# Moving work in the front of a gated attention mix: row-maximum units, weight splits, head casts and inversions at other places

## The chip, the cores and the metric

The kernel runs on one core of one Trainium2 chip. Time is device time in microseconds (us) from the first to the last instruction of one execution. The core has TensorE (PE, with its weight loads shown as PEld), VectorE (DVE), ScalarE (ACT), GpSimd (POOL) and SyncE (SP). Each engine works through its own instructions in their order and waits at semaphores. SP issues nearly all DMA transfers; the profile calls its issuing queue SPq.

## The reference, cut to what matters

There are 2048 tokens of width 448, and 16 heads of width 28. Two attention layers share the input, and a gate per token mixes them:

```python
x = A_x                                              # 1 x 2048 x 448
g = sigmoid((x * gate_w).sum(-1))                    # one gate a token
# branch A: linear attention, features by a softmax over each head's 28 columns
pq, pk = q @ w_phi, k @ w_phi                        # per head
phi = concat(softmax(p), softmax(-p))                # 56 features a head
o_a = (phi_q @ (phi_k.T @ v)) / (phi_q @ sum(phi_k) + 1e-6)
# branch B: full softmax attention over all 2048 keys
o_b = softmax(q @ k.T * 28**-0.5) @ v
out = g * (o_a @ wo_A) + (1 - g) * (o_b @ wo_B)
```

## The kernel before, in words

Operands of the projections are split into a high part (rounded to fp32r) and a low part (the rest), and each product is made of three passes: high by high, high by low, low by high. The high part is a cast, the low part a subtraction.

The program has a front, some 334 us long, and a main loop of 256 steps (lines 1123 to 1162) that does the scores, the exponentials and the values of branch B. This change lies in the front.

**The front, in order.** First come 20 projections of queries and keys for branch B (`proj_qk`, n = 4 to 19 at lines 664 to 699). Then one loop (lines 727 to 825) runs i from 0 to 42. For i below 16 it handles the keys and values of branch A for token tile t = i (128 tokens). With q = i - 16 and y = q - 1 it handles the queries of branch A, stage after stage, one tile behind the other:

- query projection `pq` of tile q (q from 0 to 15), copied out of PSUM by ACT;
- `features1` (line 438): the extremes of each head by DVE (lines 443, 444), the two differences by POOL (447) and by POOL or DVE (449); an exponential by ACT (452), one iteration later; `features2` (455): the sums and their inverse by DVE (459, 460) and the product by POOL (461);
- `turn` (515): PE transposes the features of tile y - 2, ACT copies them out (528);
- for each pair of tiles k (256 tokens, 8 pairs): `numer` (531) multiplies with the state, and `normalize1` (395) copies the result `oU` out by ACT and has SP pick the denominators out of it by DMA into `den`; `normalize2` (405) adds 1e-6 and inverts on DVE (408, 409), then SP stores the inverses to DRAM (`rd`, line 413) and loads them back, broadcast to all partitions, into `rs` (line 414); `normalize3` (418) multiplies `oU` by `rs` on DVE (420); `normalize4` (423) casts the heads on ACT (428) and subtracts on POOL (429);
- `out_a` (557): the output projection of branch A for tile y - 10, twelve passes; ACT scales it by the gate (565) and SP stores it;
- `value_b` (712): the value projections of branch B, tiles 0 to 7 inside the loop from q = 18, tiles 8 to 15 behind it (lines 915 to 925).

Pair k is summed up at y = 2k + 4, inverted at y = 2k + 5, multiplied at y = 2k + 8, cast at y = 2k + 9 and projected at y = 2k + 10 and 2k + 11.

**Maxima units.** Branch B needs a bound on the scores of each query for its exponentials. 44 units (`mx_unit`, line 259) find part of these in the front: each is four matmuls on 28 rows (line 285) into the PSUM tiles `pmb` and `pmd`, a Relu by ACT (288) and two add-and-maximum operations by DVE (290), each with a read of its accumulator. A unit's `pmb` is written where the unit before had its own, so PE waits for DVE there. Units stand between other work: at n = 16 to 19, two for each pair of key tiles (one at the start, one by `tick` at half the passes), at q = 0, 1 and from q = 8, and a second one an iteration from q = 19 (line 817) until 44 are done.

**Weight splits.** `split_weight` (line 141) casts the high part on ACT and puts the low part, a subtraction, on a list that `take_lows` empties at the next chance, on DVE unless another engine is named.

**PSUM.** Tiles of 512 columns come from the tag `s` with three buffers, plus one tile `pv` that holds the state of branch A until q = 2 (the turn from keys to queries). There the kernel before closes its PSUM pool and opens another with four `s` buffers (lines 749 to 751).

**What sets the order.** The instructions of PE, DVE, ACT and POOL run in the order in which the program writes them. SP's order is set by the framework's planner. The main loop takes its score tiles from a list of seven PSUM banks (`free`, line 935).

Of the kernel before, what the change touches and what calls it, by code (L numbers as in the profile page):

```python
# [19 lines left out]
D = 448  # L20
# [20 lines left out]
def gated_mix_kernel(ctx, tc, xT, wqkB, wvB, wvA, wkAT, wqAT, phi, woA, woB,  # L41
# [17 lines left out]

    psn = [3, 2]  # L60

    def ps_s(nm):
        return ps.tile([P, 512], F32, tag="s", name=nm, bufs=psn[0])

    def ps_pv(nm):
        return ps.tile([P, 512], F32, tag="pv", name=nm, bufs=1)
# [74 lines left out]
    def split_weight(w, raw, bs, cs, low=nc.vector, high=nc.scalar.copy):  # L141

        high(w[:, 0, bs, cs], raw)
        lows.append(lambda: low.tensor_sub(w[:, 1, bs, cs], raw, f32(w[:, 0, bs, cs])))
# [464 lines left out]
    def part_loads(key, src, n, nm):  # L609
        loads(key, lambda: load_part(src, n, nm, 0), lambda: load_part(src, n, nm, 2))  # L610

    def split_part(w, key, n, i, low=nc.vector):
        split_weight(w, raws[key][i], slice(2 * i, 2 * i + 2), slice(0, n), low)

    def splits(n):

# [47 lines left out]
    for n in range(4, NP):  # L664
        take_acts()
        if n in (4, 5):
            x_loads(n - 2)
        if n == 8:
            nc.sync.dma_start(phi_s, phi)
            load_fold(wkAT, "k")  # L670
        if n == 10:
            part_loads("wB1", wqkB[:, :, 512:896], 384, "wB1")
        splits(n + 1)
        if n == 14:
            part_loads("wvA", wvA, 450, "wvA")
            nc.sync.dma_start(sel_s, sel)
            nc.sync.dma_start(mask_s, mask)
            for v in vap:
                nc.gpsimd.memset(v[:, :, 28:32], 0.0)
                nc.gpsimd.memset(v[:, :, 28:29], 1.0)  # L680
            feats = [bd.tile([P, H, 64], F32, name=f"feat{i}") for i in range(4)]
            for f in feats:
                nc.gpsimd.memset(f[:, :, 56:], 0.0)
        if 16 <= n < 20:
            mx_unit()
        proj_qk(n, ev)
        if n in (16, 18):
            split_part(wvA_s, "wvA", 450, (n - 16) // 2)
            take_lows()
        if 12 <= n < 16:  # L690
            fold(wkA_s, "k", n - 12)
        if n == 10:
            pair_query(0, 0)
            pair_load(0, 0)
        if n == 15:
            pair_load(0, 1)
            pair_query(0, 1)
        if n in (14, 19):
            take_subs()
# [27 lines left out]
    for i in range(2 * NT + 11):  # L727
        t, q = i, i - NT
        y = q - 1
        tb = y // 2  # L730
        take_acts()
        if t < NT and t % 2 == 0:
            mx_unit()
            passes = (55 if t < NT - 4 else 44) + (4 if t >= 4 else 0)
            pace["n"], pace["at"] = 4 if t >= 4 else 0, [passes // 2]
        if q in (0, 1):
            take_exps()

        if t % 2 == 0 and 0 <= t - 4 < NT:
            kv_add(t - 4)  # L740
            kv_add(t - 3)
        if q == 2:
            bk_s.close()
            ta_s = ExitStack()
            ta = ta_s.enter_context(tc.tile_pool(name="ta", bufs=1, reuse_waits="tile"))
            stg = ta_s.enter_context(tc.tile_pool(name="stg", bufs=2, reuse_waits="tile"))
            KV = ta.tile([P, 512], F32, name="KV")
            kvT = kv_copy()
            ps_s_.close()
            ps = ps_s_.enter_context(tc.tile_pool(name="psq", bufs=1, space=PSUM, reuse_waits="tile"))  # L750
            psn[0] = 4
            woA_s = weights(3, "woA_s")
            wvB_s = weights(2, "wvB_s")
            take_exps()
        if t < NT:
            pk = ps_s(f"pk{t}")
            tok_major(pk, t, wkA_s, D, tick)
            fk[t] = features1(pk, f"k{t}", nc.gpsimd)
            take_exps(1)
        if 0 <= q < NT:  # L760
            pq = ps_s(f"pq{q}")
            tok_major(pq, q, wqA_s, D)
        if q == 0:
            fk[NT - 1] = features2(fk[NT - 1], f"k{NT - 1}")
        if q in (1, 2):
            fq[q - 1] = features2(fq[q - 1], f"q{q - 1}")
        if 0 <= q < NT:
            fq[q] = features1(pq, f"q{q}", nc.vector if 0 < q < 9 else nc.gpsimd)
        if 0 <= t - 1 < NT - 1:
            fk[t - 1] = features2(fk[t - 1], f"k{t - 1}")  # L770
        if q in (0, 1) or q >= 8:
            mx_unit()
        if y >= 9 and y % 2 and tb - 4 < 8:
            oTs[tb - 4] = normalize4(ta, num.pop(tb - 4), f"a{tb - 4}", 2)
        if y >= 4 and y % 2 == 0 and tb - 2 < 8:
            numer(tb - 2)
        if q > 0:
            take_exps(int(q < NT))
        if q == 3:
            kv_out(kvT)  # L780
        if 2 <= q - 1 < NT:
            fq[q - 1] = features2(fq[q - 1], f"q{q - 1}")
        take_subs()
        if t == 1:
            pair_load(0, 3)
        if y >= 8 and y % 2 == 0 and tb - 4 < 8:
            num[tb - 4] = normalize3(*num[tb - 4], 2)
        if t < NT:
            value_a(t)
            if t % 2 and t < NT - 4:  # L790
                proj_qk(NP + t // 2, ev)
        if q in (0, 1):
            proj_qk(NP + 6 + q, ev)
        take_lows()
        if 2 <= i < 6:
            fold(wqA_s, "q", i - 2)
        if q == 1:
            ev_s.close()
        if q == 2:
            raws["woA"] = [load_woA(b) for b in (0, 2)]  # L800
        if q == 11:
            part_loads("wvB", wvB, D, "wvB")
        if q in (4, 6):
            split_part(woA_s, "woA", D, (q - 4) // 2)
        if q in (14, 17):
            split_part(wvB_s, "wvB", D, (q - 14) // 3)
        if q == 1:
            gates()
        if y < 9 or y % 2:
            if y >= 2 and y - 2 < NT:  # L810
                turn(y - 2)
        if 0 <= y - 10 < NT:
            out_a(y - 10)
            out_a2(y - 10)
        if y >= 9 and y % 2 == 0 and y - 2 < NT:
            turn(y - 2)
        if NT + 3 <= q < NT + 10:
            mx_unit()
        if q == NT + 2:
            bd_s.close()  # L820
            vb = [value_tile(0)]
        if 0 <= q - NT - 2 < 8:
            value_b(q - NT - 2)
        if y >= 5 and y % 2 and tb - 2 < 8:
            num[tb - 2] = normalize2(ta, *num[tb - 2], f"a{tb - 2}", 2, True)
    ta_s.close()
    wp_s.close()
    vb.append(value_tile(1))
# [80 lines left out]
    ps_s_.close()  # L909
    ps = ps_s_.enter_context(tc.tile_pool(name="psv", bufs=1, space=PSUM, reuse_waits="tile"))  # L910
    psn[:] = 2, 3
    rlp = fr_s.enter_context(tc.tile_pool(name="rlp", bufs=1, reuse_waits="tile"))
    mx_unit()
    rest = NF - mxs["u"]
# [17 lines left out]

    free, used, held = list(range(7)), [], []
    spare = []

    def bank(i, nm):
# [292 lines left out]
```

## Time and profile before

| | |
|---|---|
| three runs | 1019.61, 1020.08 (median), 1020.7 us |
| profiled execution | 1018.93 us, span of its trace 1017.1 us |
| PE busy | 1006.6 us (99%) |
| ACT busy | 817.2 us (80%) |
| DVE busy | 682.1 us (67%) |
| POOL busy | 236.4 us (23%) |
| mean granted TensorE clock | 0.998 |

A row of a timeline has the start in us from the span's begin, the duration in us, the engine, the source line, the operation, and the tile written and those read; xN means that N instructions stand together. A bracket gives the time that the engine was idle just before and what ended that time. A row of the windows has busy us of PE, PEld, DVE, ACT and POOL with their instruction counts, then the granted clock of PE, the busy share of the DMA engines and GB/s. A row of one tile has the smallest, the median and the largest duration in ns, and the first and the last start. A row of waits has the total us, the times, and the longest.

### The profile page before, as it was taken

Reading aid. Unit: us, or ns where it says so; the run is one execution under the profiler, and the core shown is the slowest. Engines: PE = TensorE matmul, PEld = TensorE weight load, DVE = VectorE, ACT = ScalarE, POOL = GpSimd, SP = SyncE. Lnnn points to the kernel's source line nnn. Section 1 sums busy time; section 2 is a strip of 40 time slices with the busy share of each in tenths; the row PEclk is TensorE's granted clock in tenths of the full one; section 3 lists DMA queues with packets and bytes.
Section 4 is the critical chain, followed back from the end, with each engine's and each line's share of the span. In section 5 each row is a group of like instructions: output and inputs, shape, how many; then the busy total and the mean of one; then the engine's idle time right before and its main releaser. Section 6 shows DMA issues by size and latency. Waiting matters only on the chain.

```text
span 1017.1 us, 18036 instructions
## 1 busy us (share of the span) xinstructions
PE 1006.6 (99%) x6472; PEld 563.0 (55%) x6472; DVE 682.1 (67%) x1340; ACT 817.2 (80%) x1534; POOL 236.4 (23%) x213
## 2 busy tenths in 40 slices
PE   9999999999999999999999999999999999999998
PEld 8878888878779433333333333333333333355656
DVE  5566657997753578888887888787887878710102
ACT  5445445677753899999999999999999999978682
POOL 1235456588435102110011110101201011011010
PEclk9999999999999999999999999999999999999999
DMA  8973110132345703232522223532323345516131
GB/s 298 312 236 92 58 52 1 44 90 82 91 131 122 160 14 90 58 80 69 124 68 70 55 58 78 126 68 53 87 55 75 76 100 138 144 48 163 56 111 55
DMA packets 64250, 98.89 MB, mean 97 GB/s; under 512 B 18176, under 2 KB 24944, under 8 KB 64160
## 3 DMA queue, kind: packets, MB, share of 16 engines
q1 hardware_dynamic: 64160, 97.74, 36.0%
q8 instruction: 51, 0.84, 0.3%
q14 instruction: 39, 0.32, 0.1%
HBM read 69.54 MB, written 27.78 MB: 96 GB/s over the span
## 4 chain that ended last, share of the span: by engine, by line
PE 92%; DVE 4%; DMA 1%; ACT 1%; issue 1%; SPq 0%; POOL 0%; DVEq 0%; ACTq 0%; POOLq 0%
PE st L873 29%; PE pv L1004 25%; PE pm L322 9%; PE pqk L109 5%; PE pk L127 4%; PE pva L127 4%; PE pob L109 3%; PE poa L109 3%; PE pq L109 2%; PE pvb L127 2%; PE pvb L109 1%; PE pmb L285 1%; PE pqk L652 1%; DMA dena<-oUa 1%; PE pft L525 1%; DVE fsumq L459 1%
## 5 line engine op out<-in xcount | busy, mean ns | idle before, releaser
L895 ACT ACTIVATE p<-st 128x512 f32<-128x512 f32 x1020 | 522.8, 615 | 25.6 <-PE st L873 25.5
L333 DVE TENSOR_REDUCE part<-pm 128x1 f32<-128x512 f32 x477 | 304.8, 686 | 111.1 <-PE pm L322 104.7
L873 PE MATMUL st<-qst,kst 128*128 128x512 f32 x1024 | 310.2, 427 | 0.6 <-ACT vb L715 0.5
L1004 PE MATMUL pv<-p,vb 128*32 128x512 f32 x2048 | 268.4, 604 | 0.0
L873 PEld LDWEIGHTS st<-qst,kst 128*128 128x128 f32 x1024 | 174.6, 187 | 122.3 <-issue 59.0
L322 PEld LDWEIGHTS pm<-kc,qc 28*128 28x128 f32 x848 | 40.5, 181 | 177.8 <-ACT p L895 169.4
L326 ACT ACTIVATE rl<-pm 128x512 f32<-128x512 f32 x212 | 126.9, 599 | 11.1 <-PE pm L322 0.3
L420 POOL TENSOR_TENSOR oUb<-oUb,rsb 128x512 f32<-128x512 f32 x15 | 19.4, 1291 | 464.1 <-DMA rsb<-rdb 192.6
L330 DVE CUSTOM_DVE_ANT_0 rl<-pm,rl 128x512 f32<-128x512 f32 x159 | 108.3, 681 | 0.0
L322 PE MATMUL pm<-kc,qc 28*128 28x512 f32 x848 | 107.1, 495 | 0.0
L1004 PEld LDWEIGHTS pv<-p,vb 128*32 128x32 f32 x2048 | 44.4, 108 | 70.2 <-issue 62.0
L290 DVE CUSTOM_DVE_ANT_0 rl<-pmb,rl 128x512 f32<-128x512 f32 x88 | 57.0, 686 | 29.4 <-ACT rl L288 29.4
L1016 DVE SCALAR_TENSOR_TENSOR acc<-pob,gate,acc 128x448 f32<-128x448 f32 x12 | 8.2, 684 | 90.8 <-PE pob L109 90.8
L109 PE MATMUL pqk<-XH,wB 128*128 128x512 f32 x192 | 59.3, 397 | 0.0
L288 ACT ACTIVATE rl<-pmd 128x1024 f32<-128x1024 f32 x44 | 45.2, 1028 | 12.4 <-PE pmd L285 6.0
L589 ACT CAST ev<-pqk 128x512 fp32r<-128x512 f32 x28 | 16.0, 589 | 37.3 <-PE pqk L109 32.5
L109 PE MATMUL poa<-woA_s,oTa 128*128 128x448 f32 x192 | 43.2, 374 | 0.0
L109 PEld LDWEIGHTS pqk<-XH,wB 128*128 128x128 f32 x192 | 35.4, 188 | 8.5 <-issue 1.5
L196 POOL TENSOR_TENSOR kc<-kc,kd 28x512 fp32r<-28x512 f32 x12 | 15.4, 1281 | 101.3 <-PE pm L322 60.2
L109 PE MATMUL pq<-wqA_s,XH 128*128 128x448 f32 x128 | 37.8, 378 | 0.8 <-DVE ev L590 0.8
L590 DVE TENSOR_TENSOR ev<-pqk,ev 128x512 fp32r<-128x512 f32 x28 | 19.0, 690 | 29.2 <-ACT ev L589 29.1
L109 PEld LDWEIGHTS poa<-woA_s,oTa 128*128 128x128 f32 x192 | 35.1, 188 | 5.9 <-issue 3.3
(161 smaller groups left out, 1178.0 us busy)
## 6 DMA issues: line engine op xcount, KB each, us to landing
qkd<-ev SPq DMA_DIRECT2D x28, 512.0 KB
qst<-qkd SPq DMA_DIRECT2D x64, 224.0 KB
kst<-qkd SPq DMA_DIRECT2D x64, 224.0 KB
od<-oTb SPq DMA_DIRECT2D x48, 112.0 KB
rsa<-rda SPq DMA_DIRECT2D x8, 512.0 KB
rsb<-rdb SPq DMA_DIRECT2D x15, 256.0 KB
kc<-qkd SPq DMA_DIRECT2D x64, 56.0 KB
gad<-ga SPq DMA_DIRECT2D x16, 224.0 KB
```

Of the source, the lines that this page charges most:

```text
L109: nc.tensor.matmul(dst, l, r, start=i == 0, stop=i == len(todo) - 1)
L127: nc.tensor.matmul(dst[:, :n], l, r, start=i == 0, stop=i == len(todo) - 1, skip_group_check=True)
L288: nc.scalar.activation(rl, pd, AF.Relu)
L290: nc.vector.tensor_tensor_reduce(rl[:, i, :], pb[:, i, :], rl[:, i, :], 1.0, LOWEST, ALU.add, ALU.max, part[:, col + i:col + i + 1])
L322: nc.tensor.matmul(pm[j], mxs[("qc", gq)][js, qt * P:(qt + 1) * P], mxs[("kc", g, kb)][js, :], start=True, stop=True, tile_position=(32 * ...
L326: nc.scalar.activation(rl, pm[kb], AF.Relu if kb < 3 else AF.Copy)
L330: nc.vector.tensor_tensor_reduce(r, pm[j], r, 1.0, LOWEST, ALU.add, ALU.max, part[:, col + j:col + j + 1])
L333: nc.vector.tensor_reduce(part[:, col + j:col + j + 1], pm[j], AX.X, ALU.max)
L420: (nc.gpsimd if n == 1 else nc.vector).tensor_mul(oU, oU, rs)
L873: nc.tensor.matmul(st, kst_of[(g, kt // 4)][:, j, (kt % 4) * P:(kt % 4 + 1) * P], qst_of[gq][:, j, :], start=True, stop=True)
L895: nc.scalar.activation(p, st, AF.Exp, scale=SCALE)
L1004: nc.tensor.matmul(pv[32 * j:32 * j + 32, :], vb[kt // 8][:, kt % 8, 4 * g + j, :], pt[j], start=kt == 0, stop=kt == NT - 1, tile_position ...
```

## The change

- **Maxima units.** Each of the key iterations t = 4, 6, 8 gets two units among its passes instead of one (at a third and two thirds). The units at q = 8, 9, 10 and the second ones from q = 19 go. One unit stands behind the loop and two among the last values of branch B, where the code for that already is (lines 913 to 927).
- **PSUM.** The pool is not closed at q = 2. Instead every fourth tile is taken from `pv`, which is free by then, so four buffers rotate.
- **Weight splits.** `wvA` is cast and subtracted by POOL (before: ACT and DVE). The low parts of `woA` go from DVE to POOL. The two parts of `wvB` are split at q = 16 and 17 (before: 14 and 17).
- **Heads.** `normalize4` moves behind `turn` in its iteration for y = 11, 13, ...; at y = 9 it stays. On ACT the casts now come behind the exponential and the copies of the transposed features; on POOL the two subtractions come behind the product of `features2`.
- **Inversions.** `normalize2` of pair k moves from the end of the iteration y = 2k + 5 to y = 2k + 6, right behind `normalize3` of pair k - 1.
- **Banks.** The main loop's list of banks starts as 0, 2, 3, 4, 5, 1, 6.

```diff
+    turn4 = []
     def ps_s(nm):
+        if turn4:
+            turn4.append(nm)
+            if len(turn4) % 4 == 0:
+                return ps_pv(nm)
         return ps.tile([P, 512], F32, tag="s", name=nm, bufs=psn[0])
...
-            split_part(wvA_s, "wvA", 450, (n - 16) // 2)
+            split_part(wvA_s, "wvA", 450, (n - 16) // 2, nc.gpsimd, nc.gpsimd.tensor_copy)
...
-            pace["n"], pace["at"] = 4 if t >= 4 else 0, [passes // 2]
+            pace["n"] = 4 if t >= 4 else 0
+            pace["at"] = [passes // 3, 2 * passes // 3] if t in (4, 6, 8) else [passes // 2]
...
-            ps_s_.close()
-            ps = ps_s_.enter_context(tc.tile_pool(name="psq", bufs=1, space=PSUM, reuse_waits="tile"))
-            psn[0] = 4
+            turn4.append("")
...
-        if q in (0, 1) or q >= 8:
+        if q in (0, 1) or q >= 11:
             mx_unit()
-        if y >= 9 and y % 2 and tb - 4 < 8:
+        if y == 9:
             oTs[tb - 4] = normalize4(ta, num.pop(tb - 4), f"a{tb - 4}", 2)
...
         if y >= 8 and y % 2 == 0 and tb - 4 < 8:
             num[tb - 4] = normalize3(*num[tb - 4], 2)
+        if y >= 6 and y % 2 == 0 and tb - 3 < 8:
+            num[tb - 3] = normalize2(ta, *num[tb - 3], f"a{tb - 3}", 2, True)
...
-            split_part(woA_s, "woA", D, (q - 4) // 2)
-        if q in (14, 17):
-            split_part(wvB_s, "wvB", D, (q - 14) // 3)
+            split_part(woA_s, "woA", D, (q - 4) // 2, nc.gpsimd)
+        if q in (16, 17):
+            split_part(wvB_s, "wvB", D, q - 16)
...
+        if y >= 11 and y % 2 and tb - 4 < 8:
+            oTs[tb - 4] = normalize4(ta, num.pop(tb - 4), f"a{tb - 4}", 2)
         if 0 <= y - 10 < NT:
             out_a(y - 10)
...
-        if NT + 3 <= q < NT + 10:
-            mx_unit()
...
-        if y >= 5 and y % 2 and tb - 2 < 8:
-            num[tb - 2] = normalize2(ta, *num[tb - 2], f"a{tb - 2}", 2, True)
...
-    free, used, held = list(range(7)), [], []
+    free, used, held = [0, 2, 3, 4, 5, 1, 6], [], []
```

More of the change, by code (lines that the diff above doesn't have):

```diff
@@ L610, in part_loads, with split_part @@
         loads(key, lambda: load_part(src, n, nm, 0), lambda: load_part(src, n, nm, 2))
-    def split_part(w, key, n, i, low=nc.vector):
-        split_weight(w, raws[key][i], slice(2 * i, 2 * i + 2), slice(0, n), low)
+    def split_part(w, key, n, i, low=nc.vector, high=nc.scalar.copy):
+        split_weight(w, raws[key][i], slice(2 * i, 2 * i + 2), slice(0, n), low, high)
     def splits(n):
@@ L911, in gated_mix_kernel @@
     psn[:] = 2, 3
+    turn4.clear()
     rlp = fr_s.enter_context(tc.tile_pool(name="rlp", bufs=1, reuse_waits="tile"))
```

## The prediction

> **What bounds the kernel now.** The page's engine rows come first, then the table of windows over the front, then PE's timeline with its idle times.
>
> ```profile
> PE 1006.6 (99%) x6472; PEld 563.0 (55%) x6472; DVE 682.1 (67%) x1340; ACT 817.2 (80%) x1534; POOL 236.4 (23%) x213
> ...
> 110.00:120.00 10.00, 10.00 (x51) 8.51 (x50) 6.26 (x12) 4.99 (x9) 6.36 (x6) 1.00 0.05 14
> 200.00:210.00 10.00, 10.00 (x89) 8.06 (x87) 9.66 (x16) 9.14 (x15) 7.82 (x6) 1.00 0.18 49
> 210.00:220.00 10.00, 7.88 (x65) 5.68 (x63) 9.79 (x21) 5.16 (x10) 7.53 (x6) 0.83 0.40 115
> ```
>
> PE is the bound, and all that could be won in the front is its idle time. The windows say where: between 210 and 220 PE works 7.88 of 10 us and the granted clock falls to 0.83, while DVE is full in both query windows (9.66 and 9.79). In the key stage (110 to 120) DVE has room.
>
> ```profile
> 56.63 0.50 PE L285 MATMUL pmd<-kp,qp 28*128 28x512 f32 x2 [0.37 <-DVE part L290]
> 63.85 0.49 PE L285 MATMUL pmd<-kp,qp 28*128 28x512 f32 x2 [0.33 <-DVE part L290]
> 184.18 0.68 PE L109 MATMUL pq<-wqA_s,XH 128*128 128x448 f32 x2 [0.82 <-DVE ev L590]
> 213.61 0.50 PE L285 MATMUL pmd<-kp,qp 28*128 28x512 f32 x2 [2.12 <-DVE part L290]
> 260.40 0.50 PE L285 MATMUL pmd<-kp,qp 28*128 28x512 f32 x2 [0.57 <-DVE part L290]
> 279.30 0.50 PE L285 MATMUL pmd<-kp,qp 28*128 28x512 f32 x2 [0.23 <-DVE part L290]
> 289.46 0.50 PE L285 MATMUL pmd<-kp,qp 28*128 28x512 f32 x2 [0.46 <-DVE part L290]
> 337.14 0.96 PE L873 MATMUL st<-qst,kst 128*128 128x512 f32 x3 [0.48 <-ACT vb L715]
> ```
>
> These waits sum to 5.38 us; the clock at 213 costs 0.17 x 10 = 1.7 more. So 7.1 us is about all that can be gained.
>
> **The change part by part.** The main loop keeps its instructions; it starts earlier or later.
>
> *wvA to POOL.* DVE loses two subtractions and ACT two casts between 53 and 63 us, the cause of the first two waits: -0.70. POOL waited 10.61 us there, until the second key pair's load:
>
> ```profile
> 58.03 2.66 POOL L221 TENSOR_TENSOR kp<-kp,kt 28x512 fp32r<-28x512 f32 x2 [10.61 <-DMA kt<-qkd]
> L144 POOL TENSOR_TENSOR woB_s<-woB_raw,woB_s 128x448 fp32r<-128x448 f32 x4 | 4.6, 1147 | 0.3
> ```
>
> By the second row a subtraction of 900 columns is some 2.3 us, with a cast of half that 3.4 a part, 6.8 in all: it fits if the weights are there by 51. Without that cover the pair's two subtractions come late for the unit at 63: up to +0.7 instead.
>
> *PSUM kept.* The first `pq` takes the bank used three tiles earlier instead of the one just written: the 0.82 go, -0.8 (bounds -0.82 and 0, if POOL then holds the features).
>
> *Units to the keys.* Three units move to t = 4, 6, 8. They are work moved, not added (0.43 of PE each). A unit now follows another after about 20 passes, some 4 us; DVE reaches its two operations (0.69 each) some 2.5 us after the unit, so it ends about as the next one starts: +0.2, between 0 and +1.
>
> *Units away from q = 8 to 10; woA's low parts to POOL.* This removes the 2.12 and its clock loss, if nothing else is late there. POOL takes on two subtractions of 2.3 us (the row above, doubled) in a stage where its windows show 7.8 and 7.5 of 10. So POOL is next in line; but the next part is later still, and covers it.
>
> *Inversions a tile later: the term that decides.* In the new order DVE multiplies pair k by `rs`, then adds and inverts pair k + 1, then continues. Between this inversion and the next multiplication lie a store, a broadcast load, and one pair of tiles. Before it was that pair and about half of another. These rows follow one pair, then show two more loads and the ends of the series:
>
> ```profile
> 263.65 0.35 DVE L409 RECIPROCAL dena<-dena 128x32 f32<-128x32 f32 x1
> 264.04 1.15 SPq L413 DMA_DIRECT2D rda<-dena  x2
> 267.10 0.54 SPq L414 DMA_DIRECT2D rsa<-rda  x1
> 275.73 1.23 DVE L420 TENSOR_TENSOR oUa<-oUa,rsa 128x1024 f32<-128x1024 f32 x1 [1.18 <-DMA rsa<-rda]
> ...
> 290.95 0.54 SPq L414 DMA_DIRECT2D rsa<-rda  x1
> 299.46 1.59 SPq L176 DMA_DIRECT2D kc<-qkd  x4
> SPq L176 <- DMA rsa<-rda: 2.7, 1, 2.7
> ...
> 206.09 1.18 SPq L413 DMA_DIRECT2D rda<-dena  x2
> 208.71 0.53 SPq L414 DMA_DIRECT2D rsa<-rda  x1
> ...
> 250.43 0.54 SPq L413 DMA_DIRECT2D rda<-dena  x1
> 254.23 0.54 SPq L414 DMA_DIRECT2D rsa<-rda  x1
> ...
> L408 DVE TENSOR_SCALAR dena<-dena x8: 118/884/1733, 205.6 to 287.5; 128x32 f32<-128x32 f32 x8
> L420 DVE TENSOR_TENSOR oUa<-oUa,rsa x8: 1161/1190/1226, 218.9 to 301.5; 128x1024 f32<-128x1024 f32 x8
> ```
>
> The multiplication at 275.73 had to wait although its inversion ended at 264.00: the path took 11.73 us, 8.63 of it the broadcast. The load of 290.95 freed the transfer waiting for it at 299.46, after 8.5. Store to load is 2.62 (206.09 to 208.71), 3.06 (264.04 to 267.10) or 3.80 (250.43 to 254.23). One turn of the new loop is then
>
> 1.19 (multiply) + 0.2 (add; 0.118 to 0.884) + 0.35 (invert) + 0.04 (issue) + 3.06 + 8.5 = 13.3 us,
>
> with ends 12.8 (shortest add and store) and 14.9 (median add, longest store, 8.63). The eight multiplications stood from 218.9 to 301.5 before, 82.6 us, or 11.8 a pair. So PE reaches the next pair sooner than the data. DVE then stands, and behind it in its queue the extremes, the maxima of the units (PE waits for these at the next unit), the sums that POOL needs, and `wvB`'s low parts; PE follows.
>
> The first turn: the addition of pair 0 now stands behind the sum of query tile 6:
>
> ```profile
> 207.89 1.07 DVE L459 TENSOR_REDUCE fsumq<-feat 128x32 f32<-128x896 f32 x1
> 201.33 2.43 POOL L461 TENSOR_TENSOR feat<-feat,fsumq 128x896 f32<-128x896 f32 x1 [0.72 <-DVE fsumq L460]
> L461 POOL TENSOR_TENSOR feat<-feat,fsumk 128x896 f32<-128x896 f32 x16 | 27.3, 1705 | 2.5 <-DVE fsumk L460 0.8
> L447 POOL TENSOR_TENSOR feat<-pcq,extq 128x448 f32<-128x448 f32 x16 | 17.4, 1088 | 2.3 <-DVE extq L443 2.3
> ```
>
> Its sum ends at 208.96; two inversions and the addition make 209.9. SP issues the store, and in its new order holds the second `wvB` load ahead of the broadcast; that load waits until POOL has subtracted `woA`'s second part. Counting POOL on from 201.33 (three products of 1.7, two differences of 1.0, two subtractions of 2.3: 11.7), that is 213.0, and with the load's own issue and small waits some 213.6, an estimate from these rows. Plus 8.5, the first multiplication starts at 222.1: 3.2 later than 218.9. Seven turns take 93.1 instead of 82.6: +10.5.
>
> What follows the last multiplication is shorter than before, since PE has run ahead to the next unit:
>
> ```profile
> 301.75 0.42 PE pmb L285
> 305.25 2.65 PE poa L109 x12
> 307.90 2.26 PE pvb L109 x11
> 317.33 16.73 PE pvb L127 x81
> ```
>
> Before it took 317.33 - 301.5 = 15.8. Now: 1.2 multiply, 1.45 for the unit behind it, two output projections of 2.65 and 2.45, a value tile of 2.3, two halves and a whole unit (0.9): 11.0, and 3 x 0.42 = 1.3 for the units moved behind the loop: 12.3, so -3.5. The loop in all: 3.2 + 10.5 - 3.5 = +10.2. Since it is the slower one, the waits of 213, 260, 279 and 289 give nothing of their own. The casts behind the turn, and `wvB` at 16 and 17, are priced at nothing for the same reason; if the loop were no longer than PE's pair, POOL would come to the heads only after the product of the last tile (1.7 more, by the row of line 461), and PE would stand some 2.5 us at the output projection near 261: an estimate, that product and half of the next head's subtraction.
>
> *The first bank of the main loop* is no longer the one that ACT is emptying: -0.5 (0 if another is late).
>
> Sum: -0.7 - 0.8 + 0.2 + 10.2 - 0.5 = +8.4. The profiled execution (1018.93, span 1017.1) would go to 1027.3. It lies 1.15 below the median, so on the median it is 1020.08 + 8.4 = 1028.5.
>
> The Trainium skill, page "DMA: Bandwidth & Descriptors", section "Anatomy of one DMA", gives for GpSimd's transfers 2.0 us plus bytes over 436 GB/s; by that the 512 KB would land in some 3.2 us, an estimate from that page, where the row shows 8.63 for a transfer issued by SP.
>
> **The rivals.**
>
> *The data comes in time, and the change does what its parts say (faster).* If the broadcast lands within 6.9 us instead of 8.5, a turn is 11.7, below the 11.8 of a pair, and DVE never waits. Then all waits go: -0.70 - 0.82 - 2.12 - 1.7 - 0.57 - 0.23 - 0.46 - 0.48 + 0.2 = -6.9: 1013.2. For it speaks that loads collide less when PE is slower; against it the two landings, 8.5 and 8.63. The page named above would decide this way.
>
> *The loop closes about even and POOL sets the pace.* Turns of 12.0 or so add little (7 x 0.2 + 3.2 - 3.5 = +1.1). The waits on POOL replace those on DVE: at 261 +2.5 - 0.57, and 1.7 for the clock after so long a wait; with -1.8 for the certain parts: +2.9, so 1023.0. The same rows stand against it, though less strongly.
>
> *The loop, and a slow clock besides.* If PE stands over 2 us once a pair, each wait can cost 1.7 again, as at 213. It adds where PE's own pair is as long as the turn (four pairs in the middle): 4 x 1.7 = 6.8, so 1035.3.
>
> **How the numbers follow.** Chances: the loop as computed 0.62, even loop 0.15, slow clock 0.12, in time 0.11. The time is that of the likeliest, 1028.5; its own range is 1025 to 1034 (turns of 12.8 and 14 us, 7 x -0.5 and 7 x +0.7, with the bounds of the small parts). The range for 8 in 10 reaches from 1019 to 1036, to the slow clock above and all of the even loop below, and leaves out the data in time and the slowest turns. A change of 0.2% (2.0 us) is about what can be told from none. Faster than that takes the data in time: 0.11. Within it falls part of the even loop: 0.07. Slower: 0.82.
>
> **What the next profile would show.** The multiplications of line 420's kind would each stand behind an idle time of DVE ended by `rsa<-rda`, 1 to 5 us long, with starts some 13.3 apart, the last near 314. PE would wait at `pmd` for DVE and at `poa` for POOL. The wait at 184 and the two near 60 would be gone, and DVE's share between 220 and 310 lower. Wrong would be: no wait for `rsa`, or starts 12 or less apart; then the loop is not the bound and the time falls towards 1020 or below.

## The result, and the profile after

The changed kernel takes 1033.17 us (median of 4 runs, 1030.81 to 1035.77). The kernel before, run beside it, takes 1019.85 (4 runs, 1019.05 to 1020.70). The ratio is 1.0132, with a 95% interval from 1.0117 to 1.0146: slower, by 13.3 us. The ratios here and below are not the quotient of the two medians; they differ from it by up to 0.1%. Two single executions stand far out for an unknown cause: one of e9 at 1027.06 us, which counts in its ratio, and one of e10 at 5201.67, which does not. The prediction was 1028.5 within 1019 to 1036. The direction and the range held; the sum of +8.4 was too small by 4.9. The profiled execution has a span of 1031.7, 14.6 more than before.

First the engine rows of the changed kernel's page, then its windows over the query stage. The columns of the windows are the busy time of PE, PEld, DVE, ACT and POOL, then the granted clock and the transfers.

```profile
PE 1009.7 (98%) x6472; PEld 563.5 (55%) x6472; DVE 674.8 (65%) x1336; ACT 814.6 (79%) x1532; POOL 242.6 (24%) x219
```

```profile
210.00:220.00 10.00, 9.48 (x82) 7.45 (x81) 4.98 (x9) 5.11 (x10) 9.13 (x7) 1.00 0.30 84
220.00:230.00 10.00, 2.90 (x35) 1.55 (x36) 6.03 (x12) 4.38 (x8) 4.41 (x5) 0.62 0.11 26
230.00:240.00 10.00, 10.00 (x54) 8.75 (x53) 5.78 (x14) 6.97 (x12) 6.82 (x6) 0.87 0.23 77
...
270.00:280.00 10.00, 7.75 (x37) 6.30 (x36) 2.06 (x5) 5.10 (x10) 3.85 (x3) 0.66 0.36 101
```

Before, DVE was full here (9.79 of 10 between 210 and 220). Now it is half idle (4.98), and PE works only 2.90 of 10 between 220 and 230. Both engines wait for something. PE's timeline of the changed kernel gives its waits; these are all above 0.2 us from 195 on:

```profile
208.30 1.09 PE L531 MATMUL pft<-ident,feat 128*128 128x128 f32 x8 [0.84 <-POOL feat L467]
227.10 1.96 PE L545 MATMUL pn<-fT,KV 56*32 56x256 f32 x32 [7.62 <-ACT fT L534]
259.25 2.31 PE L115 MATMUL poa<-woA_s,oTa 128*128 128x448 f32 x10 [1.11 <-POOL oTa L435]
268.23 0.50 PE L291 MATMUL pmd<-kp,qp 28*128 28x512 f32 x2 [1.46 <-DVE part L296]
272.68 4.10 PE L115 MATMUL poa<-woA_s,oTa 128*128 128x448 f32 x10 [2.25 <-POOL oTa L435]
285.22 0.47 PE L115 MATMUL pvb<-wvB_s,XH 128*128 128x448 f32 x1 [1.83 <-DVE wvB_s L150]
321.75 0.50 PE L291 MATMUL pmd<-kp,qp 28*128 28x512 f32 x2 [1.67 <-DVE part L296]
```

They sum to 16.8 us. The waits at 56, 63 and 184 are gone. The releasers are ACT, POOL and DVE, so none of these is the cause by itself. DVE's own rows show what holds DVE: the group of the eight multiplications, then the first, the fifth and the last from the timeline.

```profile
L426 DVE TENSOR_TENSOR oUa<-oUa,rsa 128x1024 f32<-128x1024 f32 x8 | 9.7, 1217 | 33.1 <-DMA rsa<-rda 32.9
...
223.33 1.23 DVE L426 TENSOR_TENSOR oUa<-oUa,rsa 128x1024 f32<-128x1024 f32 x1 [6.83 <-DMA rsa<-rda]
279.20 1.22 DVE L426 TENSOR_TENSOR oUa<-oUa,rsa 128x1024 f32<-128x1024 f32 x1 [7.94 <-DMA rsa<-rda]
319.25 1.23 DVE L426 TENSOR_TENSOR oUa<-oUa,rsa 128x1024 f32<-128x1024 f32 x1 [7.41 <-DMA rsa<-rda]
```

DVE stood 32.9 us for the broadcast, against 1.18 before. Three of PE's waits come right behind such a wait: 7.62, 1.83 and 1.67, together 11.1 us. The other four, 5.7 us, do not: the one at 208 is ahead of the first multiplication, and those at 259, 268 and 272 stand behind DVE's or POOL's queue after multiplications that found their data there. The wait of 7.62 is handed on through ACT's queue: the cast of the first head waits for the multiplication, and the exponentials of a query tile, then the copy that PE needs, are queued behind the cast.

```profile
224.58 1.14 ACT L434 CAST oTa<-oUa 128x512 fp32r<-128x512 f32 x2 [8.13 <-DVE oUa L426]
225.63 0.94 ACT L458 ACTIVATE feat<-feat 128x896 f32<-128x896 f32 x1
226.48 1.05 ACT L534 COPY fT<-pft 128x512 f32<-128x512 f32 x2
```

The chain of waits that ended last, in the changed kernel, goes through one turn like this. From here on, the loop is the round that the order makes: multiply, invert the next pair, store, broadcast, multiply.

```profile
224.47 0.19 DVE dena L414
...
224.68 0.35 DVE dena L415
...
225.66 1.92 DMA rda<-dena
...
227.66 8.30 DMA rsa<-rda
```

Between 213 and 319 us five of the eight broadcasts lie on this chain. Between 252 and 293 it runs mostly elsewhere: through the sums and the units on DVE, the head's subtraction on POOL, the copy and the picking of denominators behind it, and the store of an output tile.

All seven turns, from DVE's and SP's timelines (multiplication to issue of the store, store to load, load to the next multiplication):

| multiplication at | to the store | store to load | load to next | turn |
|---|---|---|---|---|
| 223.33 | 1.73 | 2.60 | 8.32 | 12.65 |
| 235.98 | 1.73 | 2.93 | 8.66 | 13.32 |
| 249.30 | 3.24 | 2.59 | 8.74 | 14.57 |
| 263.87 | 3.17 | 2.53 | 9.63 | 15.33 |
| 279.20 | 1.73 | 2.59 | 8.86 | 13.18 |
| 292.38 | 1.73 | 2.59 | 9.26 | 13.58 |
| 305.96 | 1.73 | 2.52 | 9.04 | 13.29 |
| mean | 2.15 | 2.62 | 8.93 | 13.70 |

Every turn is the sum of its three columns, because each column ends where the next begins. In five turns the last column ends a wait of DVE for the broadcast, so no instruction of PE is in them. In the two that end at 249.30 and 263.87 it does not: DVE came to the multiplication straight from a sum that ACT's exponential had held (2.10 and 3.45 us). There the column only says that the broadcast landed no later. The second of these, from DVE's timeline:

```profile
262.48 1.08 DVE L465 TENSOR_REDUCE fsumq<-feat 128x32 f32<-128x896 f32 x1 [3.45 <-ACT feat L458]
...
263.87 1.16 DVE L426 TENSOR_TENSOR oUa<-oUa,rsa 128x1024 f32<-128x1024 f32 x1
```

The last output projection of the loop and the first score product of the main loop, of the changed kernel, and that score product of the kernel before:

```profile
327.53 2.71 PE L115 MATMUL poa<-woA_s,oTa 128*128 128x448 f32 x12
...
348.55 0.62 PE L878 MATMUL st<-qst,kst 128*128 128x512 f32 x2
```

```profile
333.90 0.62 PE L873 MATMUL st<-qst,kst 128*128 128x512 f32 x2
```

The main loop starts 14.65 later, which is the whole difference of the spans (14.6).

### The profile page after: what moved, and what is told of

Same layout as the page of the kernel before. It is cut to its first block, busy times and chain, and to the rows that moved or that the text cites. A ratio compares the mean times of both kernels' runs of the same rounds, so it can differ in the third digit from the quotient of the medians.

```text
span 1031.7 us, 18038 instructions
## 1 busy us (share of the span) xinstructions
PE 1009.7 (98%) x6472; PEld 563.5 (55%) x6472; DVE 674.8 (65%) x1336; ACT 814.6 (79%) x1532; POOL 242.6 (24%) x219
## 4 chain that ended last, share of the span: by engine, by line
PE 87%; DMA 7%; DVE 3%; POOL 1%; issue 1%; SPq 0%; ACT 0%; POOLq 0%; DVEq 0%; ACTq 0%
PE st L878 28%; PE pv L1010 24%; PE pm L328 9%; PE pqk L115 6%; DMA rsa<-rda 4%; PE pk L133 4%; PE pva L133 4%; PE pob L115 3%; PE pvb L133 2%; PE pmb L291 1%; PE pq L115 1%; PE pqk L658 1%; DMA rda<-dena 1%; DMA gad<-ga 1%; DMA dena<-oUa 1%
## 5 line engine op out<-in xcount | busy, mean ns | idle before, releaser
L115 PE MATMUL poa<-woA_s,oTa 128*128 128x448 f32 x192 | 47.5, 398 | 3.4 <-POOL oTa L435 3.4
L115 PEld LDWEIGHTS poa<-woA_s,oTa 128*128 128x128 f32 x192 | 37.1, 203 | 11.8 <-issue 4.2
L133 PE MATMUL pva<-wvA_s,XH 128*128 128x450 f32 x128 | 37.6, 371 | 0.0
```

Source lines behind the costliest of these rows:

```text
L115: nc.tensor.matmul(dst, l, r, start=i == 0, stop=i == len(todo) - 1)
L133: nc.tensor.matmul(dst[:, :n], l, r, start=i == 0, stop=i == len(todo) - 1, skip_group_check=True)
```

## The experiments

The theory: the multiplication waits for the broadcast and the next inversion waits, in DVE's queue, for the multiplication, so the store, the broadcast and the multiplication form a loop longer than PE's pair of tiles. The main rival: POOL, with more work and with the heads behind the turn, sets the pace. Where runs are compared that did not run side by side, "by the ratios" means by their ratios to the kernel before that ran beside each of them.

**e4: the inversions alone.** The kernel before, with this one edit:

```diff
+        if y >= 6 and y % 2 == 0 and tb - 3 < 8:      # behind normalize3
+            num[tb - 3] = normalize2(...)
-        if y >= 5 and y % 2 and tb - 2 < 8:           # end of the iteration
-            num[tb - 2] = normalize2(...)
```

> The kernel before with the inversions a tile later, and nothing else of the change. Theory of the loop: multiplications 13.3 to 13.9 apart with waits for rsa of 2 to 8 us, the waits of before at 56, 63, 184 and 213 remain: 1028 to 1035, that is 8 to 15 above the kernel before. Rival, POOL and the other parts carry the loss: 1019 to 1023.

Measured: 1031.70 (1030.58 to 1033.07) against 1018.83, ratio 1.0129 (1.0112 to 1.0146). DVE's timeline of this kernel, three of the eight:

```profile
235.41 1.23 DVE L420 TENSOR_TENSOR oUa<-oUa,rsa 128x1024 f32<-128x1024 f32 x1 [2.11 <-DMA rsa<-rda]
274.95 1.23 DVE L420 TENSOR_TENSOR oUa<-oUa,rsa 128x1024 f32<-128x1024 f32 x1 [6.31 <-DMA rsa<-rda]
315.90 1.23 DVE L420 TENSOR_TENSOR oUa<-oUa,rsa 128x1024 f32<-128x1024 f32 x1 [1.43 <-DMA rsa<-rda]
```

This one part, without POOL's new work and without the moved heads, costs as much as the whole change, as the theory expected (1028 to 1035). From 222.84 to 315.90 are seven turns of 13.3; single ones go from 12.5 to 14.7, and the multiplication at 302.08 did not wait.

**e2: all but the inversions.** The changed kernel with that edit reversed.

> The changed kernel with the inversions back at their old place (end of odd y, a tile earlier); all other parts as changed. Theory of the loop: no wait for rsa over 1.5 us, multiplications 11.8 apart, the first near 218; what is left are the parts that remove waits: 1013 to 1018. Rival, POOL sets the pace: waits of PE on POOL at poa and at pn of 1 to 3 us each and the slow clock remain: 1023 to 1031.

Measured: 1018.74 (1016.14 to 1020.54) against 1018.83, ratio 1.0001 (0.9990 to 1.0012). So the place of the inversions is the whole loss, and the other parts together gain nothing. The theory's 1013 to 1018 was missed at its upper end: its waits for `rsa` are gone (1.93 once), but PE has new ones:

```profile
206.72 1.09 PE L531 MATMUL pft<-ident,feat 128*128 128x128 f32 x8 [0.46 <-POOL feat L467]
215.27 1.09 PE L531 MATMUL pft<-ident,feat 128*128 128x128 f32 x8 [0.96 <-POOL feat L467]
222.30 1.29 PE L545 MATMUL pn<-fT,KV 56*32 56x256 f32 x32 [3.28 <-ACT fT L534]
263.15 3.30 PE L115 MATMUL poa<-woA_s,oTa 128*128 128x448 f32 x10 [1.87 <-POOL oTa L435]
```

Two of them decide. At 222.30 it is again the cast of the first head in ACT's queue: it waits for the first multiplication, that for its broadcast. Before, a unit's wait of 2.12 at 213 held PE back just ahead of it; that PE now arrives early and stands here instead is the likely reading. At 263.15 it is the head's subtraction on POOL behind the product of tile 15. Run e6 takes the first of these waits away, run e5 the second. The rows of DVE, ACT and POOL from the timeline of this kernel:

```profile
217.98 1.77 DVE L426 TENSOR_TENSOR oUa<-oUa,rsa 128x1024 f32<-128x1024 f32 x1 [1.93 <-DMA rsa<-rda]
...
219.79 1.14 ACT L434 CAST oTa<-oUa 128x512 fp32r<-128x512 f32 x2 [3.85 <-DVE oUa L426]
...
260.18 1.70 POOL L467 TENSOR_TENSOR feat<-feat,fsumq 128x896 f32<-128x896 f32 x1 [1.19 <-DVE fsumq L466]
261.83 2.52 POOL L435 TENSOR_TENSOR oTa<-oUa,oTa 128x512 fp32r<-128x512 f32 x2
```

**e1: the loop opened by one exchange.** The changed kernel, two calls swapped; the orders of PE, ACT and POOL stay.

```diff
+        if y >= 6 and ...: num[tb - 3] = normalize2(...)   # pair k + 1: add, invert
         if y >= 8 and ...: num[tb - 4] = normalize3(...)   # pair k: multiply
-        if y >= 6 and ...: num[tb - 3] = normalize2(...)
```

> The changed kernel with the two calls of one pair exchanged: the addition and inversion of pair k + 1 stand ahead of the multiplication of pair k instead of behind it. Orders of the other engines stay. Theory of the loop (the multiplication waits for the broadcast, and the next inversion for the multiplication): the loop is open, so a wait no longer delays the next broadcast. Seven turns fall from 13.7 to PE's pair of about 11.8, with waits for rsa below 1 us from the second on. The first wait stays (its broadcast is issued at 213.64, behind the second wvB load), with the 7.6 us of PE at 227 and the slow clock behind it. Time about 1024, between 1021 and 1027. Rival, POOL sets the pace (woA's low parts and the heads' subtractions behind the products): POOL's order is unchanged, so 1031 to 1034.

Measured: 1026.72 (1025.89 to 1027.80) against 1018.83, ratio 1.0083 (1.0068 to 1.0098).

```profile
222.33 1.23 DVE L426 TENSOR_TENSOR oUa<-oUa,rsa 128x1024 f32<-128x1024 f32 x1 [6.07 <-DMA rsa<-rda]
232.34 2.62 DVE L426 TENSOR_TENSOR oUa<-oUa,rsa 128x1024 f32<-128x1024 f32 x1
...
273.20 1.23 DVE L426 TENSOR_TENSOR oUa<-oUa,rsa 128x1024 f32<-128x1024 f32 x1 [3.25 <-DMA rsa<-rda]
285.76 1.16 DVE L426 TENSOR_TENSOR oUa<-oUa,rsa 128x1024 f32<-128x1024 f32 x1
```

The last multiplication now starts at 309.34: seven turns of 12.4 in place of 13.70. The order of two instructions of one engine is worth 0.5%, with POOL's order untouched. That speaks for the loop and against the rival. The first wait stays, as expected; waits of 3.25 and 1.53 (the last) stay too, which was not expected, and 1026.72 lies at the upper end of 1021 to 1027. The other 8.4 us of the loss remain. Part of them is the start: the first multiplication comes at 222.33, against 217.98 in e2.

**e3: the broadcast spread.** The changed kernel with its order kept; only the transfer is written in another way (the edit is shortened).

```diff
-        nc.sync.dma_start(rs, rd.unsqueeze(1).to_broadcast([4, 32, n * 512]))
+        for h in range(4):                                  # n == 2 only
+            nc.sync.dma_start(rs[32 * h:32 * h + 32], rd[h:h + 1].to_broadcast([32, n * 512]))
```

> The changed kernel, all its order kept, with the broadcast of a pair's reciprocals written as four transfers of 32 partitions by 1024 values instead of one of 128 partitions read as 4 rows by 32. In the trace of the changed kernel the transfer runs at 0.25 of the transfer engines and about 90 GB/s for some 6 us. If that quarter comes from the four rows, the new form spreads and lands in 3 to 5 us, 1.3 us of issue included. Theory of the loop: a turn is then about 9, below PE's 11.8, so from the second multiplication on none waits over 1 us, and the first wait falls from 6.8 to about 2: 1015 to 1020. Rival, the loop is not the bound: time stays at 1031 to 1034 although the transfer is shorter. If the form does not spread, landing stays at 8 to 9 and nothing is told apart.

Measured: 1022.84 (1021.98 to 1024.38) against 1018.83, ratio 1.0046 (1.0031 to 1.0061). One window in the middle of a broadcast, of the changed kernel and then of this one (the last two columns are the share of the 16 transfer engines and GB/s):

```profile
245.00:246.00 1.00, 1.00 (x7) 0.82 (x6) 0.58 (x2) 0.34 (x1) 1.00 (x2) 1.00 0.25 90
```

```profile
214.00:215.00 1.00, 1.00 (x7) 0.74 (x6) 0.82 (x1) 1.00 (x3) 1.00 (x2) 1.00 0.97 366
```

SP's issue of a later pair and the multiplication that waits for it, from the timeline of this kernel:

```profile
263.96 1.72 SPq L421 DMA_DIRECT2D rsa<-rda  x4
268.16 1.23 DVE L426 TENSOR_TENSOR oUa<-oUa,rsa 128x1024 f32<-128x1024 f32 x1 [2.55 <-DMA rsa<-rda]
```

One transfer of four rows keeps a quarter of the engines busy; four transfers keep nearly all of them, and where DVE waits for the data it is there 4.1 to 5.6 after the first issue, where it took 8.3 to 9.7. The Trainium skill, page "DMA: Bandwidth & Descriptors", section "Why a DMA increments its semaphore by 16 and not by 1", says why: a transfer uses as many engines, up to 16, as divide the slowest dimension of both its patterns; here that is 4, and 32 (so 16) in the new form. The shares of 0.25 and 0.97 agree. The estimate from that page in the prediction (3.2) is far from the slow form, and nearer to the spread one: in the rows above 4.2 from the first issue, 2.5 from the end of the issues (265.68 to 268.16).

The time falls by 0.9%, with no order changed: the length of the broadcast is in what bounds this stage. It is not all of it. The expected 1015 to 1020 was missed by 3, and "no wait over 1 us" by the 2.55 above and one of 2.13. Seven turns take 87.8, or 12.5 each, although the round itself is shorter: from 258.21 to 268.16 it takes 9.95. The expectation set the round against the mean pair of 11.8, but the pairs are uneven: in e2 the same two multiplications are 7.3 apart. PE still waits 3.50 at 222 on ACT's queue and 2.31 at 267 on POOL's, as in e2, and 1.46 at 262 for a unit on DVE, which e2 does not have.

**e5: the heads back as well.** As e2, and `normalize4` for all odd y from 9 ahead of the turn, as before.

```diff
-        if y == 9:
+        if y >= 9 and y % 2 and tb - 4 < 8:
             oTs[tb - 4] = normalize4(...)
-        if y >= 11 and y % 2 and tb - 4 < 8: ...            # behind the turn
```

> As e2_inv_back (the changed kernel with the inversions at their old place), and also the casts and subtractions of the heads at their old place, ahead of the turn, for all odd y from 9 on. In e2_inv_back PE waits 1.87 us at 263.15 for POOL's subtraction of a head, which stands behind the product of tile 15, and the granted clock falls to 0.83 in that stretch (1.7 us). Theory: that is the price of this part, so both go: 3.0 to 3.6 below e2_inv_back, 1015 to 1016. Rival: another wait takes its place, as the low parts of wvB on DVE did at 260 in the kernel before (0.57): gain below 1 us.

Measured: 1016.27 (1016.12 to 1018.00) against 1019.12, ratio 0.9966 (0.9953 to 0.9980), so 0.35% (3.6 us) below e2 by the ratios, as expected. The wait of 1.87 on POOL is gone; one of 0.58 stands there:

```profile
260.67 1.15 PE L545 MATMUL pn<-fT,KV 56*32 56x256 f32 x32 [0.58 <-ACT fT L534]
```

**e6: e2 with the broadcast spread**, the edit of e3.

> As e2_inv_back, with the broadcast in four transfers as in e3_spread. In e2_inv_back the first multiplication waits for its broadcast until 217.98 (issued at 208.45), ACT's cast of the first head waits for it 3.85 us with the exponentials of a query tile behind it, and PE stands 3.28 us at 222.30 with a clock of 0.83 behind that. Theory: the first broadcast sets this wait, whatever wait is removed ahead of it. With a landing of 4 to 5.6 us the first multiplication starts near 214, and PE's wait and the slow clock go: 4 to 5 below e2_inv_back, 1014 to 1015. Rival: POOL's queue (products behind woA's low parts) sets it: PE's wait stays over 2 us and the gain is below 1.5.

Measured: 1016.37 (1015.96 to 1017.12) against 1019.12, ratio 0.9964 (0.9950 to 0.9977). The 3.28 at 222 became two smaller waits:

```profile
221.09 1.15 PE L545 MATMUL pn<-fT,KV 56*32 56x256 f32 x32 [0.73 <-ACT fT L534]
224.08 2.34 PE L115 MATMUL poa<-woA_s,oTa 128*128 128x448 f32 x10 [1.23 <-POOL oTa L435]
```

By the ratios that is 3.8 below e2, a little less than the expected 4 to 5. The first broadcast was what set the wait of 3.28. But the first multiplication starts at 217.30 and not near 214: it comes straight behind a sum on DVE, and POOL is what PE meets next. And not all of the 3.8 need be this wait: e2's profile has a granted clock of 0.83 in two windows, e6's in none, although its 1.87 at 262 is still there.

Together e2, e3 and e6 and the changed kernel also say how much of the loss hangs on the broadcast. With the long transfer the late inversions cost 13.3 us (1.0132 against 1.0001), with the spread one still 8.4 (e3 against e6, 1.0046 against 0.9964). What makes up these 8.4 was not separated. In e3 the multiplications behind the first still wait 5.5 us for their data, and three windows of 10 us have clocks of 0.66, 0.76 and 0.90, where e6 has 1.00.

**e7: both.** Inversions and heads at their old places, the broadcast spread.

> e5 and e6 together: inversions and heads at their old places, broadcast in four transfers, the rest of the change kept. If the two waits are independent, the gains add: 7 to 8.5 below e2_inv_back, 1010 to 1012, 0.7 to 0.9 percent below the kernel before. If one only moves the other: 1014 to 1016.

Measured: 1013.50 (1013.34 to 1014.17) against 1019.12, ratio 0.9936 (0.9922 to 0.9950). By the ratios the gains are 3.6 and 3.8 alone and 6.6 together, a little under the expected 7 to 8.5: the two waits are nearly independent, as far as intervals of 1.4 us to either side can tell. This beats both kernels. It is 6.5 below the kernel before (5.6 by the medians). The prediction had counted 6.9 for the case in which no new wait appears, but that the numbers are close confirms nothing: PE still waits 0.46, 0.97, 0.72, 1.22 and 0.58 here, and it took undoing two parts of the change and one edit that the change does not have.

**e8: three small parts alone.** The kernel before with wvA's split on POOL, the PSUM set kept, and the order of the first banks, as in the change.

```diff
-            split_part(wvA_s, "wvA", 450, (n - 16) // 2)
+            split_part(wvA_s, "wvA", 450, (n - 16) // 2, nc.gpsimd, nc.gpsimd.tensor_copy)
...
-            ps_s_.close()
-            ps = ps_s_.enter_context(tc.tile_pool(name="psq", ...)); psn[0] = 4
+            turn4.append("")
...
-    free, used, held = list(range(7)), [], []
+    free, used, held = [0, 2, 3, 4, 5, 1, 6], [], []
```

> The kernel before with three parts of the change alone: wvA's split on POOL, the PSUM set kept, and the order of the first banks. By the sum of the prediction these remove the waits of 56, 63, 184 and 337: -0.70 - 0.82 - 0.48 = -2.0, so 0.2 percent below the kernel before, 1016.8 where that takes 1018.8. Rival: the time won ahead of the query stage is lost again at the wait of 213, where the first head's broadcast sets the end: 0 to -0.5.

Measured: 1017.72 (1015.71 to 1021.26) against 1019.12, ratio 0.9983 (0.9971 to 0.9996), so -1.7. The waits of 56, 63 and 184 are gone. That of the first bank is not, though the order of banks is the new one:

```profile
335.12 0.96 PE L877 MATMUL st<-qst,kst 128*128 128x512 f32 x3 [0.48 <-ACT vb L721]
```

**e9: the kernel before with the broadcast spread, alone.**

> The kernel before with only the broadcast in four transfers. Before, one multiplication in eight waited for its broadcast (1.18 us at 275.73), and no wait of PE is put down to it. Theory: the transfer was hidden there, and became the bound by the later inversion alone: 0 to -1.0 against the kernel before. Rival: the shorter transfer is worth by itself what it was worth in e3_spread (about 10) or in e6 (2 to 3), since it sets the first head in every order: -2 to -3.

Measured: 1017.74 (1017.17 to 1027.06) against 1018.45, ratio 1.0001 (0.9985 to 1.0016); the medians are 0.7 apart. The transfer was hidden before, whatever its length. The same edit is worth 0.9% where the loop is closed (e3), 0.4% in e6, and nothing here.

**e10: woA's low parts back on DVE**, from e7.

```diff
-            split_part(woA_s, "woA", D, (q - 4) // 2, nc.gpsimd)
+            split_part(woA_s, "woA", D, (q - 4) // 2)
```

> As e7_both, with woA's low parts back on DVE. In e7_both PE waits 0.46 and 0.97 us for POOL's products behind these two subtractions (2.3 us each), then 0.72 and 1.22 near 220. Theory: POOL's queue is what is next in line there, so with the subtractions on DVE (1.05 us each, and the units are gone from this stage) most of the 3.4 us goes: 1.5 to 3 below e7_both, 1010.5 to 1012. Rival: DVE, full to 9.6 of 10 there, is late in its place: 0 to 2 above e7_both.

Measured: 1014.37 against 1018.45 (five of six runs 1013.96 to 1015.02), ratio 0.9956 (0.9944 to 0.9969): 0.2% above e7 by the ratios, at the edge of what can be told. The expected gain did not come. The waits at 207 and 215 became one:

```profile
216.56 1.63 PE L531 MATMUL pft<-ident,feat 128*128 128x128 f32 x8 [2.33 <-POOL feat L467]
```

POOL's product before it starts at 214.81, right behind DVE's sum and its inverse (end 214.66). DVE was late because its second subtraction took 2.62 (from 208.63) where 1.05 was expected. So the change's placing of these subtractions is, if anything, the better one.

**e11: e8 with the broadcast spread.** It differs from e7 in the units, in woA's low parts and in wvB's.

> e8_small_parts with the broadcast in four transfers; it differs from e7_both in the units (old place, also q = 8 to 10), in woA's low parts (DVE) and in wvB's (old tiles). Its wait of 2.0 us at 211 is for a unit's second operation on DVE, so the shorter transfer does not touch it: 0 to 1 below e8_small_parts, 1016.5 to 1017.7, that is 3 to 4 above e7_both: this is then what moving the units is worth once the broadcast is short. Rival: the units' move is worth nothing, and this run comes within 1 of e7_both.

Measured: 1015.86 (1013.85 to 1017.01) against 1018.45, ratio 0.9968 (0.9956 to 0.9980), 0.3% above e7 and, by the ratios, 1.5 us below e8, where 0 to 1 was expected. PE still waits 2.00 us at 211 for a unit's second operation. So the three edits together, the units' move among them, are worth something like 3 us once the first head's data is not what PE meets next; they were not separated. Much of that can be the clock: the two executions of e11 with a mean clock of 1.000 took 1014.47 and 1013.85, where e7 takes 1013.34 to 1014.17; the other three, at 0.997 and 0.998, took 1015.86 to 1017.01.

## Why the prediction was right, and where its sizes were off

**The deciding term was the right one.** "Inversions a tile later" was given +10.2, and everything else about -1.8. e4 (1.0129) confirms the first number's place: the part alone costs as much as the whole. The rest came out as nothing (e2: 1.0001, or -1.0 to +1.2 us) and not as -1.8, because of the waits that e2 shows. Of the loss, e1 takes back 5.0 us by opening the loop and e3 8.8 by shortening the transfer, so the step was right: the round of multiplication, inversion, store and broadcast is too long. But 8.4 us remain in e1 against e2, and as many in e3 against e6. In e1 the later first multiplication, 3.2 in the sum, is a part of that; the rest is open.

**The turn: 13.70, forecast 13.3.** By columns: 2.15 up to the store where the sum had 1.78; 2.62 for store to load where it had 3.06; 8.93 for the landing where it had 8.5. The first came from two additions of 1.68 in place of 0.2, the third from a landing longer than the 8.5 and 8.63 quoted (9.02 on average in the five turns that waited for it); the second was too long. The longest turn, 15.33, is beyond the 14.9 of the sum. Seven turns gave +13.3 (223.33 to 319.25 is 95.9, against 82.6), not +10.5. This is the term that was mis-sized most.

**The first multiplication: 223.33, forecast 222.1.** The inversion (from 209.22, forecast to end at 209.9) and the issue of the broadcast behind the second `wvB` load came out to the tenth (forecast 213.6):

```profile
213.13 0.40 SPq L138 DMA_DIRECT2D wvB_raw<-in_wvB_dram  x1
213.64 0.56 SPq L420 DMA_DIRECT2D rsa<-rda  x1
```

The landing was 9.7 and not 8.5. A second error lies ahead of this point. The sum added -1.3 for the early parts, but in this execution nothing of it had reached the query stage: POOL's product of line 467 starts at 201.31, where it started at 201.33. PE's starts say why. The execution began 0.5 late: its first eight projections took 3.12 (2.87 before, 2.08 in e2), so the next began at 8.05 instead of 7.56. From there the parts on `wvA` and on PSUM gave 1.4 and 0.9 back, where 0.7 and 0.8 were forecast. But from the first `pk` to the first `pq` it is 108.86 (63.31 to 172.17), against 107.02 before, 106.98 in e8, which leaves the units alone, and 108.92 in e2. So the three units moved to the keys cost 1.84 ahead of the query stage, 0.6 each, where the sum had +0.2. They were called work moved, not added; but what PE then saves comes later, where the loop sets the time.

**The end: -3.1, forecast -3.5.** From the last multiplication to the main loop it is 29.30, against 32.40 before (301.5 to 333.90). With +4.45 for the first multiplication and +13.3 this makes the 14.65.

**The first bank**, forecast -0.5: the new order alone does not remove its wait. e8 and e11 have that order and still wait 0.48. The wait is gone in the kernels that also move the units; which edit removes it was not separated. Nor does it show in the time: from the first score product to the end of the span it is 683.2 before and 683.15 in the changed kernel.

**What the waits that vanish are worth.** The text gave the waits of 213, 260, 279 and 289 no value, because the loop would be slower. That was right for a second reason, of which it named half in a rival: without the loop (e2) PE meets the first head's data (3.28) and POOL's queue (1.87) in their place. That rival had POOL's queue only, with 2.5 and 1.7 for the clock; e2 has 1.87 with a clock of 0.83, and e5, which removes it, gains 3.6.

**The other rivals.** The data did not come in time: DVE waited for it at six of the eight multiplications, 2.56 to 7.94 each. A slow clock did come, 0.62 and 0.87 from 220 to 240 and 0.66 from 270 to 280. By windows of 1 us it is low from 222 to 233 and from 270 to 277. The turns that hold these stretches end at 235.98 and 279.20, both with DVE idle for the broadcast (2.56 and 7.94), so PE's clock lengthened neither. That speaks against the rival's step that a slow clock adds to the loop.

**Where PE would wait** was forecast at `pmd` and `poa`. These waits came (1.46, 1.67, 1.11, 2.25), but the largest, 7.62, stands at `pn`, through the cast in ACT's queue. What stands behind a waiting multiplication was counted for DVE's own queue only, not for the queues of its readers.

## What to carry to other kernels

When an operation is moved so that one engine issues the request for the next piece right behind the use of the last, add up the whole way round: use, request, transfer, use. If that is longer than the pace of the bound engine, the turns pay the difference; here, swapping the two instructions took back over a third of the loss. Set the round against each of the engine's steps and not against their mean: a round of 9.95 was still too long for a pair of 7.3. Look at the share of transfer engines while a transfer runs: 0.25 during this broadcast meant that its shape, not its size, set its time. And a wait removed is worth what the next wait behind it leaves: the same edit (the spread broadcast) was worth 0, 0.4 and 0.9% in three orders.

## What the runs showed of the hardware

**The same idle time, other clocks.** A wait of PE of about 2 us sometimes cost the clock and sometimes not. Two kernels with a wait of 1.87 at the same place (263.15 in e2, 261.93 in e6); the windows that hold it, of e2 and then of e6, with the granted clock in the third column from the right:

```profile
260.00:270.00 10.00, 8.13 (x65) 6.45 (x51) 6.59 (x12) 7.55 (x14) 4.17 (x3) 0.83 0.25 80
```

```profile
260.00:270.00 10.00, 8.05 (x47) 6.74 (x47) 6.82 (x14) 7.94 (x16) 3.95 (x4) 1.00 0.33 91
```

The kernel before and e9 differ in the same way: 2.12 and 2.11 at 213, clocks 0.83 and 1.00 between 210 and 220. So the 1.7 us that the prediction charged for a clock after such a wait is a chance, not a price. Nor is it always seen in the time: the three executions of e8 with a mean clock of 1.000 took 1015.71 to 1016.02 and the others 1017.52 or more, but the five of the kernel before, of 47 in all, took 1018.36 to 1019.46, about its medians (1018.45 to 1019.12). The Trainium skill, page "TensorE: Matmul & The Clock Gate", section "What's actually happening", tells of a window of some 3.4 us that runs freely; that the outcome varies agrees with it, that 1.87 us can be enough is less than it states.

**An addition of 32 columns that takes 1.68.** In the third and fourth turn DVE's addition took 1.68 where it took 0.17 in the others. Beside it a product ran on POOL, itself longer than its 1.70. From the timelines of DVE and POOL of the changed kernel:

```profile
250.45 1.68 DVE L414 TENSOR_SCALAR dena<-dena 128x32 f32<-128x32 f32 x1
...
249.33 2.76 POOL L467 TENSOR_TENSOR feat<-feat,fsumq 128x896 f32<-128x896 f32 x1 [1.90 <-DVE fsumq L466]
```

The product starts 0.03 after the multiplication and ends at 252.09; the addition ends at 252.13. The Trainium skill, page "SBUF — State Buffer", section "Who interferes with whom", has DVE and POOL share a pair of ports that one instruction holds to its end; these rows agree. So the multiplication delays POOL by about its own length (2.76 against 1.70), and POOL then delays the addition, which is inside the loop.
